# Row sums of an attention stored as they lie, and read with a step of seven words in the final scaling

## The chip, the cores and the metric

The kernel runs on one core of one Trainium2 chip. The metric is device time in microseconds (us) of one execution; a smaller number is better. Several executions are timed and the median is given; one further execution runs under the hardware profiler, and all rows of "the profile" come from that one.

The core has five instruction queues that run beside each other, each strictly in its own order: PE (matmul, with a row PEld for loading its weights), DVE (vector), ACT (scalar and activation), POOL (GpSimd) and SP, which here does nothing but issue DMAs. An instruction that waits for another engine holds up all that stands behind it in its own queue.

## The reference

```
def attention(q, k, v, g_q, g_k):              # 8 batches, 12 heads, 448 rows, 64 columns
    q_n = q / sqrt(mean(q*q) + 1e-6) * g_q      # likewise k_n
    scores = q_n @ k_n.T / sqrt(64)
    attn = exp(scores - max(scores))            # row by row
    attn = attn / (sum(attn) + 1e-9)
    return attn @ v
x = attention(...).transpose(0, 2, 1, 3).reshape(3584, 768)
h = x @ w_in                                    # 768 -> 2048
return (h * cos(h)) @ w_out                     # 2048 -> 768
```

## The kernel before

**Pairs.** Two heads make a pair: 48 pairs `u`, six to a batch. A pair has 896 query rows, held as seven tiles of 128 rows (`t` = 0 to 6) on the 128 partitions. For each tile PE makes the scores `S` (L448), DVE their row minimum (L457), and ACT the exponentials `P` with their row sums as a by-product (L466). The row sums of a pair lie in the small tile `sm`: row `p` of tile `t` at partition `p`, column `t`. ACT adds 1e-9 (L474) and DVE takes the reciprocals, 128x7 numbers (L476).

**The product with v.** `P` is turned by PE in four column chunks `kc` of 128 keys: seven 128x128 transposes into the PSUM tile `PT` (L493), which ACT and DVE copy out as `hi` and `lo` (L502, L504, L512, L514). PE then multiplies with `vs` into `O` (L525, or L533 for the pairs 0 to 8). `O` lies the other way round: head and column on the partitions, the 448 query rows of a head along the free axis. So the division by the row sum needs the reciprocals along the free axis, the same on all 64 partitions of a head.

**How the reciprocals get there.** Beside the transposes of chunk `kc = 1` PE also turns the 128x7 reciprocals into a 7x128 corner of `PT` (L495); DVE copies that corner to `rt` (L479); SP stores `rt` to DRAM in `rs_d` (L482), where now all 896 numbers stand in the order of the query rows; two DMAs read 448 of them each and spread them over 64 partitions into `rs` (L351, the helper `spread`). The scaling then multiplies by `rs`: on DVE straight from `O` for the pairs 0 to 8 (`x_out`, L543), on POOL in place in `xf` for the other 39 (`x_norm`, L559). Both read 448 words that lie side by side.

**The rest.** Each batch's six `xf` are split into two parts in the tile `xs` (high part on ACT, low part on POOL, L570), and PE multiplies them with `w_in` into `ph` (L584 to L586), which ACT copies out (L596) and SP stores. All this is interleaved with the attention of the next batch, up to about 930 us of the profile. From there on the remaining part of the program handles the last batch's product with `w_in`, the cosine and the product with `w_out` (L612 to L691).

**What sets the order.** Nothing is ordered by hand. Every step is given to a planner (`Plan`, `add(engine, cost, due, function, ...)`) with a cost, a due time and the tiles it reads and writes; the planner runs a list schedule over the five engines, and each engine gets its instructions in that fixed order. `RING` says how many buffers a tile name has. A changed cost, due time or dependence can so move steps that have nothing to do with it. The steps that the change touches are added in `attend(u)`: the turn with `transp` (its part `("pt", 0, 2)` of `PT`), `rs_copy`, `rs_store`, `rs_load`, `x_out` and `x_norm`.

## Time and profile before

| | us |
|---|---|
| median of 3 runs | 1415.53 (1412.54 to 1417.36) |
| the profiled execution, its own time | 1417.64 |
| the profiled execution, span of its instructions | 1415.70 |

| in the profile | busy us | share of the span |
|---|---|---|
| PE | 1369.6 | 97% |
| DVE | 1025.7 | 72% |
| ACT | 994.8 | 70% |
| POOL | 925.4 | 65% |

"Busy" is the union of the engine's instructions; for PE, whose matmuls overlap, it is not the same as PE at its peak. A row of waits names who waited, for whom, how long in total, how often, and the longest. In a row of groups the numbers behind the bar are the busy time in us, the mean of one instruction in ns, and the engine's idle time just before such instructions with what ended it.

### The profile page before, as it was taken

The page shows a single profiled execution, that of the slowest core. Times are in us where ns is not written, and L with a number is a line of the kernel's source. Part 1 is how long each engine was busy: PE and PEld are TensorE (multiplying, and loading weights), DVE is VectorE, ACT ScalarE, POOL GpSimd, SP SyncE. Part 2 cuts the span into 40 slices and gives each one's busy share as a digit, 9 for nine tenths or more (in the row PEclk, how much of TensorE's full clock was granted, in tenths as well). Part 3 has the DMA queues.
Part 4 walks back from the last instruction along what each step waited for, and adds up shares of the span by engine and source line. Part 5 has one row for each costly group of instructions (what it writes and reads, how often), then busy time and mean ns, then how long its engine had stood idle before and what let it go on. Part 6 is the DMA issues. An engine that isn't in the chain of part 4 may idle for free. (4 is left out here: it accounts for less than half of the span.)

```text
span 1415.7 us, 22384 instructions
## 1 busy us (share of the span) xinstructions
PE 1369.6 (97%) x7361; PEld 1155.0 (82%) x7361; DVE 1025.7 (72%) x1649; ACT 994.8 (70%) x2058; POOL 925.4 (65%) x722
## 2 busy tenths in 40 slices
PE   6899989999999999999999999999999999999998
PEld 3446778888888878888888888889899899899898
DVE  6877997677778777878687755447867966867921
ACT  5777768778777867777767766456677786777741
POOL 4657779767977969896665663111575676676674
PEclk9999999999999999999999999999999999999999
DMA  6688534556658566676556542169389389389372
GB/s 215 212 250 265 161 113 136 176 173 199 213 199 248 175 210 206 200 230 194 189 156 202 170 137 80 61 215 347 104 277 342 118 294 325 117 294 337 108 238 102
DMA packets 154452, 282.62 MB, mean 200 GB/s; under 512 B 31760, under 2 KB 102368, under 8 KB 154336
## 3 DMA queue, kind: packets, MB, share of 16 engines
q1 hardware_dynamic: 154336, 281.20, 62.2%
q8 instruction: 58, 0.95, 0.3%
q14 instruction: 58, 0.48, 0.1%
HBM read 218.24 MB, written 62.89 MB: 199 GB/s over the span
## 5 line engine op out<-in xcount | busy, mean ns | idle before, releaser
L584 PE MATMUL ph<-xs,wi 128*128 128x448 f32 x768 | 291.6, 380 | 4.2 <-ACT he L596 4.0
L585 PE MATMUL ph<-xs,wi 128*128 128x448 f32 x768 | 281.0, 366 | 0.3 <-POOL xs L570 0.3
L586 PE MATMUL ph<-xs,wi 128*128 128x448 f32 x768 | 281.1, 366 | 0.0
L466 ACT ACTIVATE P<-S,sm 128x448 f32<-128x448 f32 x336 | 212.7, 641 | 76.5 <-DVE sm L457 69.8
L660 PE MATMUL y<-glo,wo 128*128 128x448 f32 x672 | 247.1, 368 | 7.8 <-POOL glo L644 7.8
L659 PE MATMUL y<-ghi,wo 128*128 128x448 f32 x672 | 246.8, 367 | 0.5 <-ACT ghi L646 0.5
L661 PE MATMUL y<-ghi,wo 128*128 128x448 f32 x672 | 246.6, 367 | 0.0
L504 ACT CAST hi<-PT 128x448 fp32r<-128x448 f32 x312 | 152.0, 537 | 80.3 <-PE PT L493 36.1
L457 DVE TENSOR_REDUCE sm<-S 128x1 f32<-128x448 f32 x322 | 184.5, 611 | 13.6 <-PE S L448 13.2
L493 PEld LDWEIGHTS PT<-ident,P 128*128 128x128 f32 x1344 | 152.4, 140 | 51.0 <-DVE lo L512 12.0
L493 PE MATMUL PT<-ident,P 128*128 128x128 f32 x1344 | 182.3, 275 | 7.2 <-DVE hi L502 3.7
L512 DVE TENSOR_TENSOR lo<-PT,hi 128x448 fp32r<-128x448 f32 x234 | 134.6, 615 | 73.0 <-ACT hi L504 71.7
L584 PEld LDWEIGHTS ph<-xs,wi 128*128 128x128 f32 x768 | 144.2, 188 | 39.8 <-issue 12.4
L585 PEld LDWEIGHTS ph<-xs,wi 128*128 128x128 f32 x768 | 144.5, 188 | 12.1 <-POOL xs L570 1.4
L586 PEld LDWEIGHTS ph<-xs,wi 128*128 128x128 f32 x768 | 144.2, 188 | 12.3
L660 PEld LDWEIGHTS y<-glo,wo 128*128 128x128 f32 x672 | 126.7, 188 | 20.1 <-POOL glo L644 9.2
L659 PEld LDWEIGHTS y<-ghi,wo 128*128 128x128 f32 x672 | 126.6, 188 | 11.7 <-ACT ghi L646 0.9
L661 PEld LDWEIGHTS y<-ghi,wo 128*128 128x128 f32 x672 | 126.6, 188 | 10.9
L304 POOL TENSOR_TENSOR r<-r,nhalf 128x14 f32<-128x14 f32 (+1 forms) x50 | 127.1, 2543 | 12.0 <-DVE r L322 8.7
L448 PE MATMUL S<-khi,qhi 64*128 64x448 f32 x399 | 107.4, 486 | 3.2 <-ACT khi L341 2.3
L525 PE MATMUL O<-hi,vs 128*128 128x448 f32 x312 | 102.3, 386 | 2.1 <-DVE hi L514 1.7
L596 ACT COPY he<-ph 128x448 f32<-128x448 f32 x128 | 68.2, 533 | 40.5 <-PE ph L586 28.8
(225 smaller groups left out, 2722.4 us busy)
## 6 DMA issues: line engine op xcount, KB each, us to landing
wo<-wo_d SPq DMA_DIRECT2D x88, 768.0 KB
h_d<-he SPq DMA_DIRECT2D x128, 224.0 KB
hb<-h_d SPq DMA_DIRECT2D x64, 448.0 KB
wo_d<-wv SPq DMA_DIRECT2D x56, 384.0 KB
sd<-sd SPq DMA_DIRECT2D x46, 448.0 KB
vd<-v SPq DMA_DIRECT2D x78, 160.0 KB
qd<-qT SPq DMA_DIRECT2D x48, 256.0 KB
raw<-w_in SPq DMA_DIRECT2D x16, 768.0 KB
```

The costliest lines, as they stand in the source:

```text
L304: nc.gpsimd.tensor_tensor(r, r, nhalf.broadcast_to([128, c1 - c0]), ALU.pow)
L457: nc.vector.tensor_reduce(least, d["S", t][:, :S], axis=AX.X, op=ALU.min)
L466: nc.scalar.activation(tl(u, f"P{t}", [128, S], F32, "P"), d.pop(("S", t))[:, :S], AF.Exp, bias=sm[:, 1, t : t + 1], scale=-1.0, accum_out ...
L493: nc.tensor.transpose(pt[:, t * 128 : t * 128 + 128], src, ident)
L504: nc.scalar.copy(hi, pt[:, hh * S : hh * S + S])
L512: nc.vector.tensor_tensor(lo, src, hi.bitcast(F32), ALU.subtract)
L584: nc.tensor.matmul(ph[:, :S], whi, x2[:, 0, :], start=(cc == 0), stop=False)
L585: nc.tensor.matmul(ph[:, :S], whi, x2[:, 1, :], start=False, stop=False)
L586: nc.tensor.matmul(ph[:, :S], wlo, x2[:, 0, :], start=False, stop=(cc == NCC - 1))
L659: nc.tensor.matmul(y, whi, hi, start=(k == 0 and chain < 2), stop=False, skip_group_check=chain == 2)
L660: nc.tensor.matmul(y, whi, lo, start=False, stop=False, skip_group_check=chain == 2)
L661: nc.tensor.matmul(y, wlo, hi, start=False, stop=(k == NH - 1), skip_group_check=chain == 2)
```

## The change

The turn on PE and the copy on DVE go, and with them the tile `rt` and the part `("pt", 0, 2)`. The 128x7 reciprocals are stored from `sm` as they lie, seven words of each partition, so that in `rs_d` query row `p` of tile `t` stands at `7p + t`. The tile `rs` has 896 columns in place of 448; three DMAs spread the numbers over the partitions: all 896 over the first 64, and two pieces (445 and 448 words, begun at places 451 and 4) over the other 64, so that on both halves the same view holds. The scaling reads this view with a step of seven words, in two instructions: 384 columns as 3 x 128, and 64 columns. The planner's numbers for these steps are set anew (0.62 to 0.75 on DVE, 1.22 to 1.5 on POOL, three issues instead of two, landing 7.0 instead of 6.0), and the store may stand right behind the reciprocal.

```diff
-    rs_d = dpool.tile([NU, 7, 128], F32, tag="rs_d", name="rs_d")
+    rs_d = dpool.tile([NU, 896], F32, tag="rs_d", name="rs_d")
...
-    def rs_copy(u):
-        nc.vector.tensor_copy(tl(u, "rt", [NQT, 128], F32), pt[:NQT, 896:1024])
-
     def rs_store(u):
-        nc.sync.dma_start(rs_d[u], pair[u].pop("rt"))
+        nc.sync.dma_start(rs_d[u].rearrange("(p t) -> p t", t=NQT), pair[u]["sm"][:, 3, :])
 
     def rs_load(u):
-        spread(tl(u, "rs", [128, S], F32), rs_d[u].rearrange("t p -> (t p)"))
+        dst, src = tl(u, "rs", [128, 2 * S], F32), rs_d[u]
+        for p0, c0, c1, s0 in ((0, 0, 2 * S, 0), (64, 0, S - 3, S + 3), (64, S, 2 * S, 4)):
+            row = src[s0 : s0 + c1 - c0].rearrange("(o s) -> o s", o=1)
+            nc.sync.dma_start(dst[p0 : p0 + 64, c0:c1], row.broadcast_to([64, c1 - c0]))
+
+    def x_scale(eng, x, y, u):
+        rs = pair[u]["rs"].rearrange("p (q t) -> p t q", t=NQT)
+        x3, y3 = (a[:, :384].rearrange("p (t q) -> p t q", t=3) for a in (x, y))
+        eng.tensor_tensor(x3, y3, rs[:, 0:3, :], ALU.mult)
+        eng.tensor_tensor(x[:, 384:S], y[:, 384:S], rs[:, 3, 0:64], ALU.mult)
...
-        if last:
-            nc.tensor.transpose(pt[:NQT, 896:1024], pair[u]["sm"][:, 3, :], ident)
...
-        nc.vector.tensor_tensor(xf[u], pair[u]["O", 0][:, :S], pair[u]["rs"], ALU.mult)
+        x_scale(nc.vector, xf[u], pair[u]["O", 0], u)
...
-        nc.gpsimd.tensor_tensor(xf[u], xf[u], pair[u]["rs"], ALU.mult)
+        x_scale(nc.gpsimd, xf[u], xf[u], u)
...
+        add(SP, ISS, D1 + 4, rs_store, u, r=[("sm", u, 3)], w=[("rsd", u)], land=LAND)
...
-                if kc == KTURN + 1 and hh == 0:
-                    w.append(("pt", 0, 2))
...
-            if kc == KTURN:
-                add(DVE, 0.25, dk + 1, rs_copy, u, r=[("pt", 0, 2)], w=[("rt", u)])
-                add(SP, ISS, dk + 2, rs_store, u, r=[("rt", u)], w=[("rsd", u)], land=LAND)
...
-        add(SP, 2 * ISS, D1 + 9, rs_load, u, r=[("rsd", u)], w=[("rs", u)], land=6.0)
+        add(SP, 3 * ISS, D1 + 9, rs_load, u, r=[("rsd", u)], w=[("rs", u)], land=7.0)
...
-            add(DVE, 0.62, D2 + 1, x_out, u, r=[("O", u), ("rs", u)], w=x[:1])
+            add(DVE, 0.75, D2 + 1, x_out, u, r=[("O", u), ("rs", u)], w=x[:1])
...
-            add(POOL, 1.22, D2 + 5, x_norm, u, r=[("rs", u)], w=x)
+            add(POOL, 1.5, D2 + 5, x_norm, u, r=[("rs", u)], w=x)
```

Since the planner's numbers change, the order moves on every engine from the first pairs to the end of the attention; behind it (the last 2411 of PE's rows) nothing moves. Three places follow. In the rows a name is followed by its pair and a number that the program gives to each buffer.

PE's queue at the turn of pair 25, chunk `kc = 1`; before:

```order
L493 MATMUL PT_98<-ident_88,P525_5609 128x128
L493 MATMUL PT_98<-ident_88,P625_5710 128x128
L495 MATMUL PT_98<-ident_88,sm25_5512 7x128
L584 MATMUL ph3_1_5817<-xs_455,wi1_463 128x448
L585 MATMUL ph3_1_5817<-xs_455,wi1_463 128x448
```

and now, where the transposes are L499 and the products with `vs` are L529:

```order
L499 MATMUL PT_98<-ident_88,P525_5632 128x128
L499 MATMUL PT_98<-ident_88,P625_5728 128x128
L529 MATMUL O25_1_5862<-hi25_1_1_5860,vs25_5484 128x448
L529 MATMUL O25_1_5862<-lo25_1_1_5877,vs25_5484 128x448
L448 MATMUL S26_2_5904<-khi26_5711,qhi26_5456 128x448
```

The turn (the row with `sm25`) is gone, and what follows the transposes is another of the steps that are ready there: the product with `vs` and the next scores, where a product with `w_in` stood.

POOL's queue at the change from batch 1 to batch 2, where the six low parts of `xs` are written (`xf12` to `xf17`) and the scaling of pair 18 follows; before:

```order
L570 TENSOR_TENSOR xs_455<-xf13_2914,xs_455 128x448
L570 TENSOR_TENSOR xs_455<-xf14_3168,xs_455 128x448
L570 TENSOR_TENSOR xs_455<-xf15_3399,xs_455 128x448
L570 TENSOR_TENSOR xs_455<-xf16_3634,xs_455 128x448
L570 TENSOR_TENSOR xs_455<-xf17_3899,xs_455 128x448
L375 TENSOR_TENSOR kl20_4188<-kd20_3929,khi20_4149 128x448
L559 TENSOR_TENSOR xf18_4167<-xf18_4167,rs18_4093 128x448
```

and now, where the low parts are L574 and the scaling L490 and L491:

```order
L574 TENSOR_TENSOR xs_443<-xf13_2912,xs_443 128x448
L300 TENSOR_SCALAR r28_4115<-r28_4115 128x14
L304 TENSOR_TENSOR r28_4115<-r28_4115,nhalf_94 128x14
L574 TENSOR_TENSOR xs_443<-xf14_3164,xs_443 128x448
L574 TENSOR_TENSOR xs_443<-xf15_3386,xs_443 128x448
L574 TENSOR_TENSOR xs_443<-xf16_3630,xs_443 128x448
L574 TENSOR_TENSOR xs_443<-xf17_3896,xs_443 128x448
L375 TENSOR_TENSOR kl20_4194<-kd20_3922,khi20_4145 128x448
L490 TENSOR_TENSOR xf18_4164<-xf18_4164,rs18_4016 128x384
L491 TENSOR_TENSOR xf18_4164<-xf18_4164,rs18_4016 128x64
```

The scaling has become two instructions behind the `kl` of pair 20, and the two instructions that prepare `r` of pair 28 now stand between the second and the third low part.

SP's queue around the store and the load of pair 25; before:

```order
L482 DMA rs_d_87<-rt25_5858 7x128
L351 DMA rkb28_5881<-r_d_86 64x448 x2
L360 DMA rqb29_5896<-r_d_86 64x512
L360 DMA rqb29_5896<-r_d_86 64x448
L360 DMA rqb29_5896<-r_d_86 64x64
L599 DMA h_d_84<-he3_1_5886 128x448
L397 DMA vd027_5926<-v 128x320
L273 DMA wo_d_85<-wv2_5_5893 128x768
L351 DMA rs25_5949<-rs_d_87 64x448 x2
```

and now:

```order
L479 DMA rs_d_87<-sm25_5524 128x7
L397 DMA vd126_5778<-v 128x320
L378 DMA qd28_5803<-qT 128x512
L603 DMA h_d_84<-he3_0_5801 128x448
L351 DMA rkb28_5827<-r_d_86 64x448 x2
L273 DMA wo_d_85<-wv2_2_5807 128x768
L485 DMA rs25_5853<-rs_d_87 64x896
L485 DMA rs25_5853<-rs_d_87 64x445
L485 DMA rs25_5853<-rs_d_87 64x448
```

The store now stands ahead of the loads of `vd126` and `qd28`, which it used to follow, and the load is three DMAs, ahead of those of `rqb29`, which it used to follow.

More of the change, by code (lines that the diff above doesn't have):

```diff
@@ L197, in tile_attention_moe @@
         "sd": 1, "r": 5, "rkb": 1, "rqb": 1, "kd": 1, "kl": 1, "khi": 1, "qd": 1, "ql": 2, "qhi": 2, "vd": 1, "vs": 2, "S": 4, "sm": 3, "P": 12,
-        "hi0": 2, "hi1": 3, "lo0": 1, "lo1": 2, "O": 1, "xf": 6, "rs": 1, "rt": 1, "ph": 1, "he": 2, "wf": 2,
+        "hi0": 2, "hi1": 3, "lo0": 1, "lo1": 2, "O": 1, "xf": 6, "rs": 1, "ph": 1, "he": 2, "wf": 2,
         "wx": 4, "wv": 2,
@@ L476, in rsum, with transp @@
             nc.vector.reciprocal(sm[:, 3, :], sm[:, 3, :])
-    def rs_copy(u):
-        nc.vector.tensor_copy(tl(u, "rt", [NQT, 128], F32), pt[:NQT, 896:1024])
     def rs_store(u):
-        nc.sync.dma_start(rs_d[u], pair[u].pop("rt"))
+        nc.sync.dma_start(rs_d[u].rearrange("(p t) -> p t", t=NQT), pair[u]["sm"][:, 3, :])
     def rs_load(u):
-        spread(tl(u, "rs", [128, S], F32), rs_d[u].rearrange("t p -> (t p)"))
+        dst, src = tl(u, "rs", [128, 2 * S], F32), rs_d[u]
[7 more added lines that the diff above has]
+        eng.tensor_tensor(x[:, 384:S], y[:, 384:S], rs[:, 3, 0:64], ALU.mult)
     KS = (0, 128, 320, 256)
-    def transp(u, kc, tiles, last):
+    def transp(u, kc, tiles):
         for t in tiles:
@@ L700, in tile_attention_moe @@
     WAHEAD = 100.0
-    KTURN = 1
     def base(u):
@@ L828, in attend @@
                 w = [("pt", 0, 0), ("pt", 0, 1)] if hh == 0 else [("pt", 0, 1)]
-                if kc == KTURN + 1 and hh == 0:
-                    w.append(("pt", 0, 2))
                 r = [("P", inst[t]) for t in tiles]
-                turn = kc == KTURN and hh == 1
-                if turn:
-                    r.append(("sm", u, 3))
-                    w = w + [("pt", 0, 2)]
-                add(PE, 0.5 if hh == 0 else 0.36 + 0.11 * turn, dk, transp, u, kc, tiles, turn, r=r, w=w, lead=0.0 if u < NP else 0.5)
-            if kc == KTURN:
-                add(DVE, 0.25, dk + 1, rs_copy, u, r=[("pt", 0, 2)], w=[("rt", u)])
-                add(SP, ISS, dk + 2, rs_store, u, r=[("rt", u)], w=[("rsd", u)], land=LAND)
+                add(PE, 0.5 if hh == 0 else 0.36, dk, transp, u, kc, tiles, r=r, w=w, lead=0.0 if u < NP else 0.5)
             for hh in range(2):
```

## The prediction, made before the changed kernel was run

> **What bounds the kernel now.** First the page: the engines' shares, and the 40 slices of 35.4 us, where each digit is the busy share in tenths.
>
> ```profile
> span 1415.7 us, 22384 instructions
> PE 1369.6 (97%) x7361; PEld 1155.0 (82%) x7361; DVE 1025.7 (72%) x1649; ACT 994.8 (70%) x2058; POOL 925.4 (65%) x722
> PE   6899989999999999999999999999999999999998
> POOL 4657779767977969896665663111575676676674
> ```
>
> PE is full from the fourth slice or so, the others are not. The change touches only the attention, up to about 930 us, so I read that part in stretches. The columns are the stretch, its length, then busy time and instructions of PE, PEld, DVE, ACT and POOL, the granted clock, the DMA engines' share and GB/s.
>
> ```profile
> 0.00:40.00 40.00, 28.18 (x114) 13.38 (x114) 28.73 (x65) 24.19 (x54) 18.50 (x20) 1.00 0.69 212
> 40.00:160.00 120.00, 112.42 (x592) 63.60 (x591) 98.97 (x147) 88.91 (x206) 84.47 (x69) 1.00 0.77 238
> 160.00:400.00 240.00, 234.66 (x1362) 200.49 (x1361) 191.47 (x311) 181.24 (x415) 188.16 (x169) 1.00 0.56 169
> 400.00:640.00 240.00, 234.69 (x1346) 197.50 (x1345) 187.09 (x313) 183.12 (x430) 195.56 (x184) 1.00 0.68 208
> 640.00:930.00 290.00, 286.12 (x1651) 246.71 (x1650) 191.64 (x333) 193.84 (x469) 153.81 (x154) 1.00 0.45 144
> ```
>
> The clock is whole everywhere. From 160 to 930 us PE is idle for 5.34 + 5.31 + 3.88 = 14.5 us of 770, and from 40 to 160 us for 7.6 of 120. So what PE no longer has to do comes off the time almost whole, and what any other engine does counts only where PE then waits for it. What PE waits for there now is in the chain of waits:
>
> ```profile
> PE O L525 <- DVE lo L512: 5.5, 7, 1.5
> PE PT L493 <- DVE hi L502: 3.7, 8, 0.8
> PE PT L493 <- DVE lo L512: 1.9, 5, 1.0
> PE O L525 <- DVE hi L514: 1.7, 1, 1.7
> PE S L448 <- POOL kl L375: 0.3, 2, 0.2
> PE ph L585 <- POOL xs L570: 0.3, 1, 0.3
> ```
>
> These are mostly the copies out of `PT` (12.8 us in sum); POOL holds PE for 0.6 us, and no row has PE waiting for a DMA.
>
> **The change part by part.** *The turn on PE.* The group of L495, and from the timeline one set of seven transposes without the turn and one with it, each with the next matmul (start, length):
>
> ```profile
> L495 PE MATMUL PT<-ident,sm x48: 272/273/273, 28.1 to 906.7; 128*7 128x128 f32 x48
> ...
> 522.99 0.93 PE L493 MATMUL PT<-ident,P 128*128 128x128 f32 x7
> 523.67 0.45 PE L525 MATMUL O<-hi,vs 128*128 128x448 f32 x1
> ...
> 537.86 0.98 PE L493 MATMUL PT<-ident,P 128*128 128x128 f32 x7
> 538.68 0.27 PE L495 MATMUL PT<-ident,sm 128*7 128x128 f32 x1
> 538.71 0.45 PE L525 MATMUL O<-hi,vs 128*128 128x448 f32 x1
> ```
>
> The 273 ns of a turn overlap its neighbours, so I take ends. Without the turn the product ends 524.12 - 523.92 = 0.20 us after the seven, with it 539.16 - 538.84 = 0.32 us after; the turn costs about 0.11 us. From start to start the difference is 0.85 - 0.68 = 0.17 us, but there the seven themselves differ by 0.05. So 48 x 0.11 = 5.3 us come off PE, 8.2 at the most, and 0 if the turns stood in idle time. I take 5.3, since idle time is 2% of this part.
>
> *The copy on DVE, and the scaling of pairs 0 to 8.* Groups of DVE: the copy; the scaling as it is; a copy of 448 columns that writes side by side; and one of 448 that writes with a step of seven words.
>
> ```profile
> L479 DVE COPY rt<-PT x48: 268/279/280, 29.1 to 907.6; 7x128 f32<-7x128 f32 x48
> L543 DVE TENSOR_TENSOR xf<-O,rs x9: 606/611/624, 42.4 to 151.7; 128x448 f32<-128x448 f32 x9
> L502 DVE COPY hi<-PT 128x448 f32<-128x448 f32 x27 | 16.6, 613 | 8.5 <-ACT hi L504 8.3
> L343 DVE COPY khi<-PT x2: 951/956/961, 10.6 to 21.8; 64x448 f32<-64x448 f32 x2
> ```
>
> DVE loses 48 x 0.279 = 13.4 us. The scaling becomes two instructions: from 128 columns in 279 ns and 448 in 611 follow 1.04 ns a column, so 384 take 545 and 64 take 213, together 0.76 us, 0.15 more than before, if the step is free. If it costs a read what it costs the write of L343 (956 against 613, a factor of 1.56), they take 1.18 us, 0.57 more. Nine times that is 1.4 to 5.1 us, where DVE is 82% busy; I take 1.4, since only one of the two inputs has the step, and book it as covered: DVE saves 9 x 0.28 = 2.5 us in the same pairs. What can come from DVE's relief on PE is bounded by the waits above: at most a quarter of the 12.8 us, since one chunk of four had the copy, so 0 to -3.2 us. I take 0, as the other copies set the pace of `PT`:
>
> ```profile
> ACT hi L504 <- PE PT L495: 32.6, 26, 2.7
> ACT hi L504 <- DVE rt L479: 6.5, 17, 0.6
> ```
>
> ACT's 32.6 us end with the turn only because it is the last of eight PE instructions; without it they end with the seventh transpose, 0.11 us earlier.
>
> *The scaling on POOL, 39 pairs.* Groups of POOL from 160 to 930 us, all reading words side by side:
>
> ```profile
> L270 POOL TENSOR_TENSOR wv<-wx,wv 128x384 fp32r<-128x384 f32 x56 | 58.6, 1049 | 30.3 <-ACT wv L267 29.3 <-DMA vd<-v 0.8
> L559 POOL TENSOR_TENSOR xf<-xf,rs 128x448 f32<-128x448 f32 x39 | 48.4, 1240 | 36.7 <-DVE xf L556 36.2
> L385 POOL TENSOR_TENSOR qd<-qd,rqb 128x512 f32<-128x512 f32 x36 | 47.8, 1328 | 2.2 <-DMA rawo<-w_out 0.8 <-DMA rs<-rs_d 0.5 <-DVE sm L457 0.4
> ```
>
> From 384 and 512 columns: (1328 - 1049) / 128 = 2.18 ns a column and 212 ns for an instruction. So 384 take 1049 and 64 take 352, in sum 1.40 us, 0.16 more than now. No POOL row reads with a step. With DVE's factor of 1.56 on the whole it is 2.19 us, 0.95 more. I take 0.16, the rows of the same engine and operation, and keep 0.95 for the range: 6 or 37 us more of POOL. On the path I book 0 for it: before the scaling POOL itself sits idle for 36.2 us waiting for `xf`, so part of the excess fills idle time. [...]
>
> If POOL's cover goes, the first to feel it are the scores: `kl` and the low parts of `xs` are in the same queue. Around 470 us it has no room at all (the first three rows are POOL's, the last is PE's):
>
> ```profile
> 468.85 4.82 POOL L570 TENSOR_TENSOR xs<-xf,xs 128x448 fp32r<-128x448 f32 x4
> 473.59 1.51 POOL L375 TENSOR_TENSOR kl<-kd,khi 128x448 fp32r<-128x448 f32 x1
> 475.05 1.60 POOL L559 TENSOR_TENSOR xf<-xf,rs 128x448 f32<-128x448 f32 x1
> 475.15 0.47 PE L448 MATMUL S<-kl,qhi 64*128 64x448 f32 x2 [0.16 <-POOL kl L375]
> ```
>
> *Store and load.* Groups of SP, and the size of one load:
>
> ```profile
> L482 SPq DMA_DIRECT2D rs_d<-rt x48: 286/293/488, 29.8 to 907.9; - x48
> L351 SPq DMA_DIRECT2D rs<-rs_d x96: 444/587/1002, 33.1 to 910.6; - x96
> rs<-rs_d SPq DMA_DIRECT2D x96, 112.0 KB
> ```
>
> The store is 128 pieces of 28 bytes in place of 7 of 512, and may cost SP 0.3 to 0.6 us. The load is three issues of 0.587 us in place of two, 28 us more of SP over 48 pairs. It moves 448 KB in place of 224: 11 MB in 930 us, 12 GB/s on 144 to 238, so a DMA share of 0.56 becomes about 0.60. All of it is off the path: the store no longer waits for turn and copy but for the reciprocal, behind it stand loads for later pairs, and POOL's scaling waited for `xf`, not for `rs`. The bounds are a gain of 0 and a loss of a few times the 0.5 us that the row of L385 shows for `rs`, so I take 0.
>
> *The order.* The planner draws it anew. Neither sign can be read from the rows; the bounds are that all 14.5 us of PE's idle time vanish or that they double. I take 0 and carry a third of that, 5 us to each side, in the range.
>
> **The sum.** -5.3 (turn) + 0 + 0 + 0 + 0 = -5.3 us. Against the profiled execution's own 1417.64 (span 1415.70 and 1.94 around it) that is 1412.3; this execution lies 2.1 us above the median of the runs, so the forecast for the median is 1415.5 - 5.3 = 1410.2 us. The main case alone spans 1406 to 1414.
>
> **The rivals.**
>
> *POOL late.* The scaling with its step takes 2.19 us, and where POOL has no idle time PE waits for the whole excess. In the page's row for POOL six slices between 160 and 930 us stand at 8 or 9 tenths, 212 us; at (907.9 - 29.8) / 47 = 18.7 us a pair (the row of L482) these are 11 pairs, 11 x 0.95 = 10.5 us, less 5.3: +5.2, 1420.7 us, slower. It decides from an excess of 0.48 us a pair (11 x 0.48 = 5.3). For it speaks the `kl` at 475 us, against it the planner, which books 0.28 more for the scaling, and the 0.6 us that PE waits for POOL today. Chance 0.15, a third of it within 0.3%. [...]
>
> *The order at the changes of batch.* At two of the six the preparation of an `r` now stands between the low parts of `xs`:
>
> ```profile
> L304 POOL TENSOR_TENSOR r<-r,nhalf 128x14 f32<-128x14 f32 x35 | 91.2, 2607 | 2.4
> L300 POOL TENSOR_SCALAR r<-r 128x14 f32<-128x14 f32 x35 | 9.4, 269 | 41.1 <-DVE r L296 39.4
> ```
>
> If PE waits for it whole, 2 x 2.88 = 5.8 us eat the gain: 1416.0. Against it: the planner put it there where it saw room. Chance 0.13, a quarter of it slower by more.
>
> *More than the turn.* If half of the 12.8 us in which PE waits for the copies out of `PT` go with DVE's 13.4 us: -5.3 - 6.4 = -11.7, 1403.8 us. For it speaks that DVE leads these waits, against it that three of four chunks never had the copy. Chance 0.12.
>
> *The turn was free.* All turns stood beside idle time of PE: 1415.5. Against it stand 14.5 idle us in 770. Chance 0.07.
>
> **How the numbers follow.** 0.3% of 1415.5, 4.2 us, is about what a measurement of this kernel can tell from no change. The main case has 0.53; it lies only 1.1 us beyond that mark, so I count 0.33 as faster and 0.20 as the same. With the rivals: faster 0.33 + 0.12 = 0.45; same 0.20 + 0.05 + 0.10 + 0.07 = 0.42; slower 0.10 + 0.03 = 0.13. The range reaches down to near the third rival and up to between the second and the first: 1404.5 to 1418.5.
>
> **What the profile after would show.** Right: no row for the turn, PE's busy time 5 us lower up to 930 us and its idle time there still 30 to 38 us; DVE's busy time 10 to 13 us lower; SP's store ahead of its former place; POOL's two instructions in sum 1.4 to 2.2 us; PE waiting for POOL no more than 2 us. Wrong: rows of PE waiting for `kl` or `xs` of 5 us and more (first and second rival), waits for `lo` and `hi` halved (third), or a busy time of PE that does not fall.

## The result, and the profile after

The change made the kernel slower. Its median is 1434.4 us (1433.5 to 1435.5, 4 runs) against 1415.07 for the kernel before, timed beside it: ratio 1.0118, 95% interval 1.0086 to 1.0151. Timed again later (run e16) it took 1434.8 us, ratio 1.0128 (1.0089 to 1.0168). The forecast was 1410.2 us, with a range up to 1418.5. One execution of run e2, which took 1885 us at a mean granted clock of 0.66, is left out of the figures below.

The page of the changed kernel: span, shares, and the slices of PE, POOL and PE's granted clock.

```profile
span 1431.7 us, 22400 instructions
PE 1373.7 (96%) x7313; PEld 1157.6 (81%) x7313; DVE 1022.6 (71%) x1610; ACT 993.8 (69%) x2058; POOL 949.3 (66%) x761
PE   6889899999989999999999999999999999999998
POOL 4656778777979987895766584111485685676674
PEclk9999899999999999999999999999999999999999
```

The profiled execution took 1433.51 us. The 48 turns are gone from PE's count (7361 to 7313), yet its busy time rose by 4.1 us over the whole program: the clock row has an 8 in the fifth slice (143 to 179 us), where PE was granted 0.86 of its clock on average. The stretches, in the same columns as in the prediction, and below them the attention as a whole, after and before:

```profile
0.00:40.00 40.00, 27.12 (x108) 13.03 (x108) 28.18 (x62) 23.77 (x52) 19.40 (x22) 1.00 0.73 217
40.00:160.00 120.00, 107.62 (x544) 58.41 (x545) 89.26 (x141) 84.17 (x201) 71.31 (x57) 0.99 0.80 243
160.00:400.00 240.00, 230.65 (x1288) 193.21 (x1288) 188.57 (x286) 176.17 (x399) 197.17 (x182) 0.98 0.60 173
400.00:640.00 240.00, 231.59 (x1330) 197.98 (x1329) 190.04 (x305) 180.35 (x424) 205.74 (x196) 0.99 0.72 216
640.00:930.00 290.00, 285.55 (x1657) 246.25 (x1656) 194.97 (x328) 198.58 (x485) 167.22 (x175) 1.00 0.54 164
0.00:930.00 930.00, 882.53 (x4923) 708.88 (x4924) 691.03 (x1119) 663.03 (x1557) 660.84 (x629) 0.99 0.64 192
```

```profile
0.00:930.00 930.00, 896.07 (x5058) 721.67 (x5059) 697.90 (x1167) 671.30 (x1570) 640.50 (x593) 1.00 0.59 182
```

PE stands idle for 47.5 us of the first 930, where it was 33.9. A lower busy time is no gain here: PE has done 135 instructions fewer by 930 us, the 48 turns and 87 others that are still to come.

What PE waits for now, in the chain of waits:

```profile
PE PT L499 <- DVE lo L516: 6.5, 6, 2.9
PE ph L588 <- ACT he L600: 4.9, 4, 3.2
PE PT L499 <- DVE hi L506: 4.6, 7, 1.3
PE O L529 <- DVE lo L516: 4.5, 7, 1.2
PE O L529 <- DVE hi L518: 4.3, 3, 1.9
PE S L448 <- POOL khi L368: 2.4, 1, 2.4
PE ph L589 <- POOL xs L574: 1.8, 6, 0.5
PE S L448 <- POOL kl L375: 0.5, 2, 0.3
```

The DVE copies, 12.8 us before, are now 19.9. Waiting for `he`, the copy of the product with `w_in`, is no new wait: the kernel before has a row for it, which the prediction's list leaves out, but there no single stop is long:

```profile
PE ph L584 <- ACT he L596: 4.0, 9, 0.7
```

Between 40 us and the last transposes PE stops for 2 us and more three times in the changed kernel (2.4, 3.2 and 2.9 us) and never in the kernel before. Where the time is lost is seen by following the last transposes of each pair (the fourth `PT` group) in the profiles. The table gives how much later than before they end; in brackets PE's idle time up to there, before and after. The second profile is that of run e16:

| pair | before, us | changed | changed, second profile |
|---|---|---|---|
| 4 | 84.4 | -0.1 (17, 17) | -0.3 |
| 6 | 112.3 | +4.4 (18, 22) | +2.4 |
| 8 | 145.6 | +4.0 (18, 22) | +3.1 |
| 9 | 169.7 | +14.0 (19, 28) | +9.0 |
| 18 | 346.8 | +15.0 (23, 32) | +10.3 |
| 24 | 464.9 | +19.5 (26, 37) | +15.5 |
| 47 | 914.3 | +19.3 (33, 47) | +16.8 |

So between half and three quarters of these delays arise between 84 and 170 us, and the second part of the program, behind the attention, takes no longer than before (498.1 us against 501.4). The timeline of the changed kernel there, PE's rows with the waits and the rows they wait for (start, length):

```profile
104.60 1.36 SPq L351 DMA_DIRECT2D rkb<-r_d  x2
...
112.81 1.33 POOL L368 TENSOR_TENSOR khi<-kd,rkb 128x448 f32<-128x448 f32 x1 [2.48 <-DMA rkb<-r_d]
114.19 1.02 PE L448 MATMUL S<-khi,qhi 64*128 64x448 f32 x4 [2.38 <-POOL khi L368]
...
152.22 0.56 DVE L216 TENSOR_SCALAR wf<-raw 128x768 int32<-128x768 int32 x1 [4.02 <-POOL wi L239]
...
158.28 0.52 ACT L600 COPY he<-ph 128x448 f32<-128x448 f32 x1
158.85 0.48 PE L588 MATMUL ph<-xs,wi 128*128 128x448 f32 x1 [3.25 <-ACT he L600]
159.59 0.36 PE L588 MATMUL ph<-xs,wi 128*128 128x448 f32 x1
160.45 0.57 PE L588 MATMUL ph<-xs,wi 128*128 128x448 f32 x1
170.88 1.76 PE L499 MATMUL PT<-ident,P 128*128 128x128 f32 x7 [2.93 <-DVE lo L516]
```

At 114 us the next pair's scores wait for `khi`, and that for a small spread load that was issued at 104.6 us and landed only about 7 us after its second issue. In the kernel before the same load, the `rkb` of pair 8, stood ahead of a load of `sd` and one of `raw` (the encoded `w_in`):

```profile
99.93 1.08 SPq L351 DMA_DIRECT2D rkb<-r_d  x2
101.11 0.53 SPq L289 DMA_DIRECT2D sd<-sd  x1
101.69 0.43 SPq L205 DMA_DIRECT2D raw<-w_in  x1
```

In the changed order it stands behind such loads. The wide load of `rs` alone doesn't make this stop: in e1 and e10 below, which have it in the order of before, this `rkb` landed 4.1 to 4.3 us after each of its issues, and `khi` began at 106.6 and 105.8 us, as before (106.1). With the old load in the new order it landed after 5.6 to 7.0 us, and `khi` began at 107.1 us (e2, no stop) and at 110.8 (e9, a stop of 1.3 us). So the order opens the way to the stop, and the wide load may lengthen it. At 159 us PE waits for a copy by ACT, which stood behind a step of decoding `w_in`; DVE's part of that had waited 4 us for POOL. Each of these three stops has a cost behind it too: a product takes 0.57 us at 160.45 us, where it took 0.36 at 159.59, and from 115.5 to 119 us the granted clock was 0.51. The granted clock (the last but two of the columns) behind the other two:

```profile
160.00:163.40 3.40, 3.40 (x12) 2.95 (x12) 0.80 (x1) 2.31 (x4) 3.40 (x6) 0.52 0.27 88
170.00:177.00 7.00, 6.12 (x20) 5.60 (x21) 6.28 (x10) 3.55 (x10) 6.83 (x6) 0.51 0.74 196
177.00:183.00 6.00, 6.00 (x37) 5.03 (x36) 5.78 (x8) 4.49 (x8) 2.19 (x3) 1.00 0.56 155
```

In the profile before no half-clock stretch falls into the attention; after, there are 17.1 us of them (at 115, 160, 170 and 610 us), which at a granted clock of 0.50 cost an estimated half, 8.5 us. But stretches of half clock come and go from one execution to the next, and they don't set the slow kernels apart. Over all executions, an estimate from the mean granted clocks ((1 - clock) times the time) gives 3 to 5 us for the kernel before (0.996 to 0.998), 10 and 7 us for the changed one (0.993 and, in e16, 0.995), and 12 us for e5 (0.992), the fastest kernel of all. The sum for the attention in this profile: 14.9 us more idle time up to its last transposes (32.6 to 47.5), 8.5 us of half clock, less some 5 us for the turns: about +18.4, where the last transposes came 19.3 us later.

What the new scaling, store and load take (ns least, median, most):

```profile
L490 POOL TENSOR_TENSOR xf<-xf,rs x39: 1203/1282/2033, 190.5 to 937.8; 128x384 f32<-128x384 f32 x39
L490 DVE TENSOR_TENSOR xf<-O,rs x9: 837/854/918, 41.3 to 157.4; 128x384 f32<-128x384 f32 x9
L491 DVE TENSOR_TENSOR xf<-O,rs x9: 249/256/273, 42.0 to 158.1; 128x64 f32<-128x64 f32 x9
L490 POOL TENSOR_TENSOR xf<-xf,rs 128x384 f32<-128x384 f32 x39 | 51.9, 1331 | 38.5 <-DVE xf L560 37.2 <-POOL vs L407 1.0
L491 POOL TENSOR_TENSOR xf<-xf,rs 128x64 f32<-128x64 f32 x39 | 24.0, 616 | 0.0
L485 SPq DMA_DIRECT2D rs<-rs_d x144: 444/587/1738, 30.8 to 927.6; - x144
L479 SPq DMA_DIRECT2D rs_d<-sm x48: 319/382/512, 26.3 to 923.7; - x48
```

DVE takes 854 + 256 = 1.11 us a pair, POOL 1.331 + 0.616 = 1.95, and the store is issued in 0.38 us.

### The profile page after: what moved, and what is told of

It is laid out like the page before. It is cut to its first block, busy times and chain, and to the rows that moved or that the text cites. A ratio compares the mean times of both kernels' runs of the same rounds, so it can differ in the third digit from the quotient of the medians.

```text
span 1431.7 us, 22400 instructions
## 1 busy us (share of the span) xinstructions
PE 1373.7 (96%) x7313; PEld 1157.6 (81%) x7313; DVE 1022.6 (71%) x1610; ACT 993.8 (69%) x2058; POOL 949.3 (66%) x761
## 4 chain that ended last, share of the span: by engine, by line
PE 49%; DVE 9%; DMA 5%; ACT 3%; POOL 3%; issue 2%; SPq 1%; DVEq 0%; ACTq 0%; POOLq 0%
PE y L664 7%; PE y L665 7%; PE y L663 6%; PE ph L588 6%; PE ph L589 5%; PE ph L590 5%; PE PT L499 5%; PE O L529 4%; PE S L448 4%; DMA rawo<-w_out 2%; POOL glo L648 2%; DMA hb<-h_d 1%; DMA h_d<-he 1%; DVE lo L516 1%; ACT ghi L650 1%
## 5 line engine op out<-in xcount | busy, mean ns | idle before, releaser
L499 PEld LDWEIGHTS PT<-ident,P 128*128 128x128 f32 x1344 | 156.0, 142 | 53.3 <-DVE lo L516 12.6
L499 PE MATMUL PT<-ident,P 128*128 128x128 f32 x1344 | 183.6, 277 | 14.0 <-DVE lo L516 6.5
L590 PEld LDWEIGHTS ph<-xs,wi 128*128 128x128 f32 x768 | 145.3, 189 | 12.5
L529 PE MATMUL O<-hi,vs 128*128 128x448 f32 x312 | 104.5, 389 | 5.1 <-DVE hi L518 4.3
```

Source lines behind the costliest of these rows:

```text
L499: nc.tensor.transpose(pt[:, t * 128 : t * 128 + 128], src, ident)
L529: nc.tensor.matmul(O, st, d.pop((what, kb, hh)), start=(kc + n == 0), stop=(kc + n == 4))
L590: nc.tensor.matmul(ph[:, :S], wlo, x2[:, 0, :], start=False, stop=(cc == NCC - 1))
```

## Experiments

The planner moves thousands of steps whenever a cost or a dependence changes, so the experiments first part the *order* from the *work*. "Old order" means that each engine's instructions stand as in the kernel before, apart from those removed or added: the planner is given the old steps, and the copy step issues nothing. All ratios are to the kernel before, timed beside each group of runs, with 95% intervals; groups were timed on different chips, so ratios are compared and not times. A difference of two ratios has a half-width worked out from theirs as if they were independent.

**The new work in the old order, and the old work in the new order.**

```diff
 # e1: the changed kernel, planner's steps and costs as before
+    def rs_copy(u):
+        pass
+                add(DVE, 0.25, dk + 1, rs_copy, u, r=[("pt", 0, 2)], w=[("rt", u)])
 # e2: the changed kernel's order, scaling and load as before
+        eng.tensor_tensor(x[:, :S], y[:, :S], pair[u]["rs"][:, :S], ALU.mult)
+        spread(tl(u, "rs", [128, S], F32), rs_d[u])
```

> The changed data path (no turn, no copy, store straight from sm, three loads, reading with a step) in exactly the order of before: the planner is given the old steps, numbers and dependences, and the step of the copy issues nothing. If the redrawn order is the cause (theory A), the old order brings the time back: 1415.1 - 5.3 for the turn + 0 to 5 for the longer scaling = 1410 to 1415 us, PE idle up to 930 us back from 47 to about 33 us, and the half-clock stretches of the attention gone. If the new work itself is the cause (theory B: scaling with a step, twice the bytes to load), it stays at 1428 to 1436 us, since all of that work is still there.

> The order of the changed kernel, instruction for instruction, with the old work in it: the scaling is one instruction that reads 448 words side by side, the load is two DMAs of 448 words each. (The reciprocals then meet the wrong rows; only the time is of use.) Theory A (order): 1428 to 1435 us, as nothing of the order has changed. Theory B (new work): 1408 to 1414 us, below the kernel before by the turn.

The new work in the old order: 1424.45 us, 1.0055 (1.0028 to 1.0082). The old work in the new order: 1423.23 us, 1.0036 (1.0018 to 1.0053). Each alone gives a third to a half of the loss. In the second one 48 turns and copies are missing and nothing is dearer than before but the store's issue, by 0.09 us, so its slowness is the order's.

**Is it the planner's numbers?** First the kernel before with only the four new numbers, then the changed kernel with the four old ones.

```diff
 # e3: before.  e4: the changed kernel, with - and + exchanged
-        add(SP, 2 * ISS, D1 + 9, rs_load, u, r=[("rsd", u)], w=[("rs", u)], land=6.0)
+        add(SP, 3 * ISS, D1 + 9, rs_load, u, r=[("rsd", u)], w=[("rs", u)], land=7.0)
-            add(DVE, 0.62, D2 + 1, x_out, u, r=[("O", u), ("rs", u)], w=x[:1])
+            add(DVE, 0.75, D2 + 1, x_out, u, r=[("O", u), ("rs", u)], w=x[:1])
-            add(POOL, 1.22, D2 + 5, x_norm, u, r=[("rs", u)], w=x)
+            add(POOL, 1.5, D2 + 5, x_norm, u, r=[("rs", u)], w=x)
```

> The kernel before with nothing changed but the planner's four numbers for scaling and load (0.75, 1.5, three issues, 7.0). No instruction is added or taken away, only the order is drawn anew. Theory A says that a redrawn order alone can cost: anything from 1415 to 1440 us, with more PE idle time between 100 and 200 us if it is slower. Theory B says 1415 +- 4 us.

> The changed kernel with the old four numbers (0.62, 1.22, two issues, 6.0); the missing turn and copy and the earlier store still redraw the order. Theory A: another draw, anywhere from 1408 to 1440 us, and its time follows its PE idle time and half-clock stretches, not the work. Theory B: 1432 to 1437 us, as the work is that of the changed kernel.

The first: 1415.52 us, 0.9997 (0.9976 to 1.0019), so an order can be drawn anew without a loss. The second: 1433.49, 1.0099 (1.0072 to 1.0127), so the order that the four old numbers give is no better.

**The parts of the new work, in the old order.** e5 takes away the turn and the copy and leaves scaling and load as they were, so that the reciprocals aren't in the order of the rows: it shows what the removal alone is worth, not a kernel to use. To it e6 adds the three wide DMAs and the second scaling instruction, e7 the step of seven words on both engines.

```diff
 # e5 (to e1)
+        spread(tl(u, "rs", [128, S], F32), rs_d[u])
+        eng.tensor_tensor(x[:, :S], y[:, :S], pair[u]["rs"][:, :S], ALU.mult)
 # e6 (to e1): both halves read side by side
+        rs = pair[u]["rs"][:, 0:384].rearrange("p (t q) -> p t q", t=3)
 # e7 (to e5): 6 x 64 and 64 words with the step, loads of 448
+        rs = pair[u]["rs"].rearrange("p (q t) -> p t q", t=NQT)
+        eng.tensor_tensor(x3, y3, rs[:, 0:6, :], ALU.mult)
+        eng.tensor_tensor(x[:, 384:S], y[:, 384:S], rs[:, 6, :], ALU.mult)
```

> The order of before, with only the turn, the copy and the detour of the store gone; the scaling is one instruction over 448 words side by side and the load is two DMAs of 448, as before. (The reciprocals then meet the wrong rows; only the time is of use.) By the prediction's first term this is the kernel before less 48 x 0.11 us: 4 to 7 us faster. If the early store or the missing copy brought something else, it is 10 us faster or not faster at all.

> As the run in the old order with the turn gone, but with the three DMAs and twice the bytes of the changed kernel, and two scaling instructions that read side by side. (Reciprocals again on the wrong rows.) If the loads carry the loss that the new work brings in the old order (theory B1: 13 us between the turn alone and all of the new work), this is 8 to 13 us slower than the turn alone, with more waiting for DMAs between 40 and 200 us. If the step carries it (theory B2), it is within 3 us of the turn alone.

> As the run in the old order with the turn gone, with two DMAs of 448 words as before, but with two scaling instructions that read with a step of seven words (as 6 x 64 and 64 columns out of the 448). (Reciprocals on the wrong rows.) Theory B2: POOL's pair takes 1.9 to 2.0 us and DVE's 1.1, as in the changed kernel, and the time is 8 to 13 us above the turn alone. Theory B1: within 3 us of it.

e5: 1408.72 us, 0.9941 (0.9922 to 0.9960). This is the gain that the change was forecast to bring, and rather more of it: some 8 us against 5.3. e6: 1419.03, 1.0028 (0.9999 to 1.0056), 0.87% above e5. e7: 1414.48, 0.9993 (0.9970 to 1.0017), 0.52% above e5. Both eat the gain. In e6, beside it, stands the price of the two scaling instructions without a step:

```profile
L493 DVE TENSOR_TENSOR xf<-O,rs 128x384 f32<-128x384 f32 x9 | 4.9, 549 | 1.6 <-DMA rs<-rs_d 1.6
L493 POOL TENSOR_TENSOR xf<-xf,rs 128x384 f32<-128x384 f32 x39 | 43.1, 1104 | 38.9 <-DVE xf L563 38.0 <-POOL vs L407 0.5
L494 POOL TENSOR_TENSOR xf<-xf,rs 128x64 f32<-128x64 f32 x39 | 19.5, 500 | 0.0
```

With DVE's 64 columns (215 ns, the median) that is 0.76 us a pair on DVE and 1.60 on POOL.

**Which part of the load, which engine's step.** e10 adds to e5 the three wide DMAs alone; e13 three DMAs that move no more than the two did; e15 the step on POOL's 39 pairs alone.

```diff
 # e10 (to e5): the changed kernel's load
+        for p0, c0, c1, s0 in ((0, 0, 2 * S, 0), (64, 0, S, S), (64, S, 2 * S, 4)):
 # e13 (to e5): 448, 224 and 224 words
+        for p0, c0, c1, s0 in ((0, 0, S, 0), (64, 0, 224, S), (64, 224, S, S + 224)):
 # e15 (to e7)
+        nc.vector.tensor_tensor(xf[u], pair[u]["O", 0][:, :S], pair[u]["rs"], ALU.mult)
```

> The order of before, the turn gone, the three wide DMAs, but one scaling instruction of 448 words side by side. (Reciprocals on the wrong rows.) Between the turn alone (0.994 of before) and the wide load with two instructions (1.003) this tells bytes from instructions: at 1.001 to 1.004 the load carries the 10 us, at 0.994 to 0.996 the second instruction (0.2 us of POOL a pair) does, which I hold for the less likely.

> The order of before, the turn gone, one scaling instruction side by side, and the load split in three DMAs (448, 224 and 224 words) that together move no more than before. (Reciprocals on the wrong rows.) The wide load cost 0.8% over the turn alone (1.002 against 0.994 of before). If that is SP's third issue, this stands at 1.000 to 1.004; if it is the bytes, at 0.993 to 0.996.

> The order of before, the turn gone, the load as before, the step of seven words on POOL's 39 pairs alone; DVE's nine scalings stay one instruction side by side. (Reciprocals on the wrong rows.) With the step on both it was 0.9993, without 0.994. If POOL's 27 us more are what counts, 0.998 to 1.000; if DVE's 4.5 us in the crowded first 160 us are, 0.994 to 0.996.

e10: 1419.4 us, 1.0023 (1.0000 to 1.0046), so of e6 it is the load and not the second instruction. e13: 1415.7, 0.9999 (0.9979 to 1.0020): the third DMA alone costs 0.58% +-0.28, and for the doubled bytes 0.24% +-0.31 are left. e15: 1410.97, 0.9953 (0.9918 to 0.9987): POOL's step costs 0.12% +-0.39, so nothing that can be measured, and DVE's nine stepped scalings are left with 0.40% +-0.42 of e7's 0.52. In the stretch from 40 to 160 us, where DVE's nine and the start-up's loads fall, the rows of e5, e10 and e13, in this order (columns as above):

```profile
40.00:160.00 120.00, 112.36 (x591) 63.48 (x589) 97.27 (x140) 90.32 (x210) 87.61 (x67) 1.00 0.77 240
```

```profile
40.00:160.00 120.00, 109.06 (x573) 61.59 (x573) 92.70 (x133) 87.56 (x204) 82.48 (x65) 1.00 0.80 247
```

```profile
40.00:160.00 120.00, 110.60 (x578) 62.37 (x577) 94.98 (x137) 88.67 (x205) 85.43 (x67) 1.00 0.75 235
```

With the wide load PE loses 3.3 us of work in these 120, with the three small ones 1.8, of the 11.6 and 8.2 us that the runs show: more than the share of these 120 us in the attention's 930. These are single profiles, and e5's is that of the slowest of its ten executions. In e13 the DMA share is no higher than in e5 (0.75 against 0.77); that speaks for SP's queue, in which each further issue of `rs` (0.587 us, the median in the changed kernel) stands ahead of all loads behind it, rather than for bytes. The waits speak for it too. Added up for DVE, ACT and POOL from 40 us to the last transposes, those that a DMA ended come to 35 to 41 us in the runs with two loads in the old order (e5, e7, e15), some 2 of them for `rs`, and to 50 to 56 us in those with three (e1, e6, e10, e13), 4 to 9 of them for `rs`: of the 14 us that are added on average, 9 are waiting for other loads. The queue was not tested apart from the transfer.

POOL's step as e15 has it, beside what PE waits for there:

```profile
L490 POOL TENSOR_TENSOR xf<-xf,rs 128x384 f32<-128x384 f32 x39 | 54.1, 1387 | 36.1 <-DVE xf L560 35.7
L491 POOL TENSOR_TENSOR xf<-xf,rs 128x64 f32<-128x64 f32 x39 | 21.0, 539 | 0.0
```

POOL spends 54.1 + 21.0 = 75.1 us on it in place of 48.4, and still sits idle for 36 us waiting for `xf`. In that profile the last transposes end 5.5 us earlier than before, near the prediction's -5.3; one profile doesn't show it, since in e5's, with 17.1 us of half clock, they end 1.9 us earlier.

**Placing the words in the store.** If the store itself put the numbers in the order of the rows, neither step nor third load would be needed, but its 896 words would be 896 pieces.

```diff
 # e8 (to e5)
+        nc.sync.dma_start(rs_d[u].rearrange("(t p) -> p t", t=NQT), pair[u]["sm"][:, 3, :])
```

> A version with right results: the reciprocals are stored from sm without turn and copy, but each word is put at the place of its row (896 pieces of 4 bytes), so that the load of two times 448 words and the scaling stay as before; the order is that of before. If what helps is the turn and what costs is the wide load and the step, this is 4 to 7 us faster than before, as the turn alone. If 896 pieces are slow to issue or to land, SP's issue of the store grows from 0.3 to over 1 us, the scaling waits for rs, and it is no faster than before.

1593.05 us, 1.125 (1.1213 to 1.1287). The page of this kernel, then SP's longest waits:

```profile
DMA packets 197555, 282.61 MB, mean 178 GB/s; under 512 B 75200, under 2 KB 145472, under 8 KB 197440
...
q1 hardware_dynamic: 197440, 281.20, 72.0%
```

```profile
SPq L351 <- DMA rs_d<-sm: 182.0, 36, 8.1
```

Loads stand waiting for their stores for 182 us in all in SP's queue, in 36 waits of up to 8.1 us, and all other loads behind them. With the 43,000 additional packets the others got slower on average: those of 1792 bytes took 114 ns in place of 86, those of 6144 bytes 436 in place of 286 (means worked out from the two traces). The medians stayed at 74 and 234 ns, so it is a part of the packets that took much longer.

**Four words for each head.** Two stores of four words from each partition give each head 512 words, loaded by three DMAs; the step is then four words.

```diff
 # e14 (to e1)
+        for h in range(2):
+            nc.sync.dma_start(
+                rs_d[u][512 * h : 512 * h + 512].rearrange("(p t) -> p t", t=4), pair[u]["sm"][:, 3, 3 * h : 3 * h + 4]
+            )
+        for p0, c0, c1, s0 in ((0, 0, 512, 0), (64, 0, 256, 768), (64, 256, 512, 513)):
```

> A version with right results in the order of before: each partition's first four words are stored for the first head and its last four for the second (two stores of 16-byte pieces), so that a head's numbers are 512 words side by side; the load brings 512 words to each partition in place of 896, and the scaling reads with a step of four words. Turn alone 0.994, plus the step's 0.5%, plus a seventh of the 0.8% for the bytes: 0.999 to 1.002 of before, so no gain. If a step of four words costs less than one of seven, 0.994 to 0.997, and it is faster than both kernels.

1430.01 us, 1.0097 (1.0063 to 1.0131), 0.42% +-0.43 above e1: it saves bytes and adds one issue, and that doesn't help. The interval just reaches 0. DVE's 384 columns took 840 ns with a step of four words, and 854 with seven.

**The second rival: the low parts of `xs`.** e2's order, with the preparation of an `r` moved behind the six low parts at the two batch changes.

```diff
 # e9 (to e2): in the finished order
+            moved = [(f, a) for f, a in part if f in (st_mean, st_pow, st_store) and a[0] in us]
+            seq = seq[:first] + kept + moved + seq[last + 1 :]
```

> The new order with the old work once more, but at the changes to batch 2 and batch 4 the two instructions that prepare r (of pairs 28 and 41) are moved behind the last low part of xs; nothing else moves. (Reciprocals on the wrong rows.) In the run of the new order with the old work PE waited 4.7 us for the low parts. If these two places are what the new order costs there (second rival of the prediction): that wait falls to about 1 us and the time by 3 to 5 us, to about 1420 us. If PE waits as long for something else: no change within 2 us.

1426.92 us, 1.0064 (1.0034 to 1.0094), not faster than e2 (1.0036). PE's wait for `xs` fell from 4.6 to 1.2 us, but its wait for `kl` rose from 0.4 to 4.6.

**The half clock.** The changed kernel with 64 more transposes of `ident`, whose result nobody reads, ahead of four long stops.

```diff
 # e11
+    WARM = {(score, 8, (0,)): 14, (ffn1, 0, 5, 0): 22, (transp, 9, 1, (0, 1, 2, 3)): 20, (av, 30, 3, 0): 8}
+            for _ in range(WARM.pop((f, *a[: {score: 2, ffn1: 3}.get(f, 4)]), 0)):
+                nc.tensor.transpose(pt[:, 896:1024], ident, ident)
```

> The changed kernel, and ahead of the four PE instructions before which PE stood idle for 2.4, 3.2, 2.9 and 1.9 us in its profile (at 114, 159, 171 and 610 us) PE turns the identity into a free corner of PT 14, 22, 20 and 8 times, 64 x 0.11 = 7 us of work without use. If idle gaps of that length bring on the stretches of half clock that followed each of them, the four stretches (17 us at half clock, 8.5 us lost) go and the time falls by 4 to 8 us, to 1426 to 1430, although PE has more to do. If the stretches come from something else, nothing falls, and where the gaps are not there in a run, it is up to 7 us slower.

1442.33 us, 1.0176 (1.0130 to 1.0223): slower. In its profile the attention has one half-clock stretch of 3.4 us in place of 17.1 us in all, and its last transposes end 4.5 us earlier than the changed kernel's (929.1 against 933.6). But the second part, which the fillers don't touch, took 506.3 us against 498.1, with three such stretches. So the half clock was kept out of those places and no time was won; one profile doesn't tell why, and that any of the loss can be got back this way isn't shown.

**The planner told the truth.** The changed kernel with the measured costs.

```diff
 # e12
-            add(DVE, 0.75, D2 + 1, x_out, ...   -            add(POOL, 1.5, D2 + 5, x_norm, ...
+            add(DVE, 1.1, D2 + 1, x_out, ...    +            add(POOL, 1.95, D2 + 5, x_norm, ...
```

> The changed kernel with the planner told what the scaling measures (1.10 on DVE, 1.95 on POOL in place of 0.75 and 1.5): another order, the same work. If a wrong booking made the order bad, 1420 to 1428 us. If the order is merely another draw, anywhere from 1422 to 1440 us, and PE's idle time up to 930 us moves with it.

1423.97 us, 1.0045 (1.0011 to 1.0079). That is 0.7 to 0.8% better than the change as it is, and still slower than before. The time lies in the range of both expectations, so the run doesn't tell whether the right costs helped or a better draw.

**The changed kernel once more**, beside e13 to e15.

> The changed kernel once more, for more executions: with stretches of half clock that come and go from run to run, the runs of the other kernels spread over 10 to 17 us. If its loss is that of the sum of the parts, 1.010 to 1.018 of before; below 1.006 the first four executions were an unlucky draw.

1434.8 us, 1.0128 (1.0089 to 1.0168): the size of the loss stands.

**Where in the order?** In the profile of e2 pair 9 loses 6.5 us on the kernel before, at the first product with `w_in`, and the second tile of `w_in` has its low part at POOL's 43rd instruction in place of the 26th (42 and 25 below, counted from zero). e17 gives the 16 tiles of `w_in` their old places in the new order. e18 keeps the old order up to the last transposes of pair 10 and the new one from there.

```diff
 # e17 (to e2): steps sorted by the planner's start time
+        weight = (w_load, w_decode, w_high, w_low)
+        part = [s for s in old if s[2] in weight] + [s for s in new if s[2] not in weight]
 # e18 (to e2)
+        n = next(i for i, s in enumerate(old) if key(s)[:4] == ("transp", u, 3, (0, 1, 2, 3)))
+        return [s[2:] for s in old[:n] + [s for s in new if key(s) not in done]]
```

> The kernel has the redrawn order and the old work (one scaling instruction, two loads of 448 words, no turn), except that the 16 tiles of w_in are loaded, decoded and split at the planner's times of the order before: the second tile's low part again at POOL's 25th row in place of the 42nd. Theory that the redrawn order costs because w_in comes late: in the profile with the redrawn order alone PE stood 2.4 us for he and 3.0 us for lo at the first product with w_in (152 and 163 us), and the seventh transposes of pair 9 came 6.5 us later against the kernel before than those of pair 8. These waits go, and of the 0.95% between the two orders at least half: ratio 0.997 to 1.000. Rival, the order costs in many places or w_in's lateness is only where it shows: ratio 1.002 to 1.005 as with the redrawn order alone (1.0036).

> The old work without the turn; the order of before up to the last transposes of pair 10 (about 190 us), and from there all remaining steps in the redrawn order. If what the redrawn order costs arises in the first 200 us, as the profiles say (6.5 of 9.5 us by pair 9), the time is near that of the old order throughout (ratio 0.9941): 0.993 to 0.997. If it arises evenly along the 930 us, four fifths of the 0.95% stay: ratio 1.000 to 1.003.

e17: 1429.95 us, 1.0081 (1.0054 to 1.0108), no better than e2 but 0.45% +-0.32 worse. PE's wait for `he` fell to 0.7 us at most, from 2.4 in e2, but a stop of 4.9 us came at 120 us, behind a step of decoding `w_in` on DVE that waited for POOL, and the stop for `lo` stayed (3.9 us at 167 us). So putting `w_in` back didn't bring the time back; what its lateness alone costs isn't shown, since the edit made a new stop. e18: 1422.01, 1.0028 (1.0011 to 1.0046), as slow as e2 although it begins with the old order. Its profile keeps the pace of before up to pair 10 (-0.9 us) and is 6.4 us late at pair 12, after a stop of 3.8 us at the seam where the two orders meet (196.7 us; the seam itself may have made it) and 6.8 us of half clock:

```profile
196.66 0.74 PE L526 MATMUL O<-hi,vs 128*128 128x448 f32 x1 [3.77 <-ACT hi L505]
```

Another 3 us are lost at pair 22, as in e2. So the new order costs as much without its first 190 us; but since most of this delay arises at the seam, which neither order has, the run doesn't settle where the cost of the new order lies. No single place in it was found.

## Why the prediction was wrong, point by point

*The turn, -5.3 us: right in kind and a little small.* e5 gained 0.59% (0.40 to 0.78), 8.3 us with an interval from 5.7 to 11.0, against bounds of 5.3 to 8.2. The rival "the turn was free" falls, and so does "more than the turn" at its price: 1403.8 is a ratio of 0.9917, and e5's interval begins at 0.9922. That some of the 8.3 us came from DVE's relief isn't excluded.

*The third DMA and the wide load, booked at 0: the first step that failed.* They cost 0.82% +-0.30 (e10 against e5), 11.6 us. The prediction saw 28 us more of SP and wrote "off the path", since no row had PE waiting for a DMA and POOL's scaling waited for `xf`. It saw "loads for later pairs" behind the store and took them for harmless, with "a few times 0.5 us" as the upper bound. That covers who reads `rs`; it doesn't cover the loads that stand behind it in SP's queue. e13 puts 0.58% +-0.28 on the third DMA alone, and the engines then wait longer for loads other than `rs`. PE has no wait for a DMA of its own in these runs either: the loss reaches it through the engines that feed it, a path on which the prediction looked at one step only. That SP's queue is that path is argued from these rows, not shown apart.

*The scaling on DVE, +1.4 us, booked as covered: the price failed, the cover most likely.* A pair took 1.11 us, near the upper bound of 1.18 and not the 0.76 taken. The two instructions without a step do take 0.76 (e6), so it is the step that was mis-sized: 384 columns went from 549 to 854 ns, a factor of 1.56, just that of the row of L343 which the prediction set aside because only one of the two inputs has the step. Nine times 0.50 is 4.5 us, more than the 2.5 that the copies gave back, on an engine that was busy 82% of that stretch. e7 against e15 leaves 0.40% +-0.42 for it, 5.7 us; that interval just reaches 0.

*The scaling on POOL: the price was wrong, the cover right.* POOL took 1.95 us, 0.71 more than before and not 0.16; 27.6 us in all. The rows of POOL without a step gave 1.40, DVE's factor on the whole 2.19. e6 has the two instructions without a step at 1.60, so the split was underpriced by 0.20, and the step, 1.93 in e15, adds 0.32. That POOL's work stays hidden held in the old order: e15 with all of it is at 0.9953. So the first rival, POOL late, falls at its price, although its direction came true.

*The order, 0 +-5 us: the second step that failed.* With the old work the new order costs 0.95% +-0.26 (e2 against e5), 13.4 us; with the new work 0.7% or so (1.012 against e1's 1.0055). The bound in the prediction, PE's 14.5 idle us doubled, was about right; to carry only a third of it was not. The second rival named two places in that order, and putting them right in e9 brought nothing back. Neither did the planner's four old numbers (e4) or `w_in` at its old times (e17). Other draws of the same work lie at 1.0045 and 1.0099 (e12, e4). One stop can be traced to it in part, the 2.4 us at 114 us for an `rkb` that now stands behind larger loads; what else in the order costs stays open.

*The sum.* Turn -0.6%, load +0.8%, step +0.5% and order +0.95% make 1.7%; taken together in the old order the two parts of the new work give e1's +1.14% over e5, and with the order 1.5%, where 1.2 to 1.3% were measured. So the parts overlap; that several of them lengthen the same stops is a reading, not a measurement.

*The signs named beforehand.* PE's idle time up to 930 us was to stay at 30 to 38 us and is 47.5; PE was to wait for POOL for no more than 2 us and does so for about 4.7, of which 2.4 go back to a DMA. DVE's busy time was to fall by 10 to 13 us and fell by 3.1 (1025.7 to 1022.6), since its scaling cost more. A busy time of PE that does not fall was a sign of being wrong, and over the whole program it rose by 4.1 us. POOL's pair within 1.4 to 2.2 us and the missing row of the turn held. The half clock was in no term.

## What to carry to other kernels

Where one engine was 98% busy (PE, 755.5 of the 770 us from 160 to 930), taking work off it paid about what was computed (5.3 us computed, 8.3 measured); the time was lost in what was booked at nothing, so price each added issue in a DMA queue like SP's (here 0.58% +-0.28 of the time for one more DMA a pair, e13) by what stands behind it there, and not by who reads its data. Where a planner redraws the order, test the new work in the old order and the old work in the new order before anything else: here they lie 16 and 13 us above the pure saving, and neither amount can be read from the diff. A step of the redrawn order that looks late in the profile is not yet the cause: two such were moved (`xs`, `w_in`), each move brought other stops, and neither gave time back.

## What the runs showed of the hardware

**Half the clock behind short stops of PE.** The records of 19 profiled executions (all kernels here but e8) have stops of PE after 40 us and stretches of half clock, each 3.41 us long or a multiple, but for the last one of each profile, at its very end. Of stops of 1.0 to 1.6 us 6 in some 110 have such a stretch during the stop or within 3.4 us behind it, of 1.6 to 2.0 us 27 in 69, of 2.0 to 2.5 us 13 in 26, of 2.5 to 3.4 us 19 in 25, and all 5 longer ones. So 32 of the 51 stops of 2.0 to 3.4 us go with half clock, and the length of a stop alone doesn't decide it. In the changed kernel's profile the stops of 2.38, 3.25, 2.93 and 1.91 us (at 114, 159, 171 and 610 us) have stretches of 3.41, 3.41, 6.83 and 3.41 us; in the one of the kernel before a stop of 2.61 us (1019 us) has one of 3.41, and one of 2.13 us (1335 us) has none. Where a stop is followed by one stretch, that costs an estimated 1.7 us on top, half of 3.41, as the clock granted there is 0.50.

**On DVE a step cost about the same with four words and with seven.** There 384 columns with one input of two read with a step took 840 and 854 ns, and 549 side by side (e6). On POOL the step added 0.32 us a pair to 1.60.

**A store in pieces of four bytes (e8).** 896 pieces of four bytes a store, 0.06% of the bytes, made the whole kernel 12.5% slower; SP's issue of such a store, 0.45 us where the changed kernel's took 0.38, shows little of it.
